# Wider weight loads in sixteen small matrix products, and seven more loop slots in written order

## The chip, the cores and the metric

The kernel runs on one NeuronCore of a Trainium2 chip. Its engines work side by side and meet only through semaphores: TensorE (PE, matrix products; the loading of its weights is listed apart as PEld), VectorE (DVE), ScalarE (ACT), GpSimd (POOL) and SyncE (SP, which issues most transfers). Each engine takes its own instructions strictly one after the other, in an order that is fixed when the program is built. The metric is the device time of one execution in microseconds; lower is better.

## The reference

Attention for 8 batches x 8 heads (512 local and 32 global positions each, 64 numbers a position), and then a two-layer network on all 4352 positions:

```python
s_l = scale * [q_l @ k_g.T, where(|i - j| <= 32, q_l @ k_l.T, -1e9)]   # local rows see a band and the 32 global keys
s_g = scale * q_g @ [k_g, k_l].T                                       # global rows see all keys
out = softmax(s) @ [v_g, v_l]          # for both
x = out rearranged to [B * 544, 512]
h = max(x @ w_in, 0)                   # 512 -> 2048
y = (h * h) @ w_out                    # 2048 -> 512
```

## The kernel before

The attention is cut into 128 tiles t: 16 groups of 256 query positions (half a batch), times 8 heads. The network is cut into 17 blocks of 256 positions with 8 steps m each (16 blocks of local positions; the last one holds the global positions). One loop (line 587) runs over both: its pass t, called **slot t** here and counted from 0, does the attention of tile t and finishes tile t-1, and does step m = t - 9 of the network. So slot 10 is the eleventh.

Tiles 0 to 15 are "plain" (line 82): their products take 32-bit numbers directly, which PE does in two passes a product. From tile 16 on, and from network block 1 on, every number is split into a high and a low part and each product becomes three; DVE and ACT make those parts.

A slot's work, in the order of the program text (lines 587 to 694): PE transposes the probabilities of tile t-1 (`pt`), does the first half of the network's first product (`h`, line 605); ACT copies `pt` (for plain tiles into `pts`, line 206); DVE masks the scores of tile t and takes their maximum (`softmax1`, a custom instruction in the profile, `prob<-s,con`); ACT does the exponentials (`softmax2`); the place 0 of the weight work; PE does the second half of `h` and the value products of tile t-1 (`av`, `xa<-pts,raw`), and for plain tiles the scores `s` of tile t+1; ACT does `relu` and `square` on `h` (`act1`, `r<-h` and `r<-r`) and copies the values out (`x_evac`, `x_h<-xa`), DVE takes the rest of them (`x_l`); DVE makes the reciprocal of the sums and ACT multiplies by it (`softmax3`; tiles 9 to 15 on ACT, line 192); place 1 of the weight work; for tile 16 on, `split_head(t+1)` (ACT `hi`, DVE `lo` and `hi`, line 125); place 2; the network's second product `o` of step m-1 on PE; place 3.

**Weight work.** The 32 weight chunks (512 KB each) come in by SP and must be unpacked: ACT makes `wf` from the raw words (`w_abs`, one instruction that is called "unpack" below, `wf<-wr`), DVE two steps on it (`w_bits`: a TENSOR_SCALAR and a SCALAR_TENSOR_TENSOR), and later ACT and DVE split the chunk for the later blocks (`w_split`: ACT `ws<-wf`, called "cast" below, DVE the remainder `ws<-wf,ws`). `PLAN` (line 30) says for each slot how many halves of `w_bits` (b) and how many splits (s) stand in its four places: slots 9 and 10 have eight b, slots 11 to 13 eight b and three or four s, slot 14 five b and four s, slots 15 and 16 five s, slots 17 to 22 two s each.

**What sets the order.** A scheduling layer orders the instructions on each engine when the program is built. `InOrder` (line 42) marks instructions so that they keep the order of the program text on their engine; `FREE = (17, 17, 17)` (line 31, used in line 589) says from which slot on this is so for DVE, ACT and PE. Before it, the layer may place an instruction where it likes, as long as the data allow it.

**Single buffers.** `pt`, `s` (from tile 8 on), `gs` and `xa` have one PSUM buffer each (line 78, `bufs=1`): the scores of tile t+1 can only be written when `softmax1` of tile t has read its own, and the next `pt` only when ACT has copied the last one.

Of the kernel before, what the change touches and what calls it, by code (L numbers as in the profile page):

```python
# [7 lines left out]
F32 = mybir.dt.float32  # L8
# [8 lines left out]
P = 128  # L17
HALF = 256
# [9 lines left out]
NPLAIN = 16  # L28

PLAN = [",,,b", "b,,,b", "b,,,b", "b,,b,", "b,,b,", "b,,b,", "b,,b,", "b,b,,b", "b,b,,b", "bb,bb,bb,bb", "bb,bb,bb,bb", "bbs,bb,bbs,bbs", "bbs,bbs,bbs,bbs", "bbs,bbs,bbs,bbs", "bbs,bbs,bs,s", "ss,s,s,s", "ss,s,s,s", "s,,s,", "s,,s,", "s,,s,", "s,,s,", "s,,s,", "s,,s,"]  # L30
FREE = (17, 17, 17)
LOOK = 2
SQ = (2, 3, 4, 5, 14, 15)
MUL = 9
# [24 lines left out]
def attention_moe(  # L59
# [18 lines left out]
    ps_a = ctx.enter_context(tc.tile_pool(name="ps_a", bufs=1, space=PSUM))  # L78
# [3 lines left out]
    def plain(t):  # L82
        return t < NPLAIN
# [141 lines left out]

    def av(t):
        hd = heads[t]
        xa = ps_a.tile([64, HALF], F32, tag="xa", name=f"xa{t}")
        c = QC + KC
        if plain(t):  # L230
            v, pts = hd["raw"][:, c:], hd["pts"]
            mm = [
                (xa, v[:, 192:256], pts[:, 256:512]),
                (xa[:, 0:128], v[:, 0:64], pts[:, 0:128]),
                (xa[:, 128:256], v[:, 64:128], pts[:, 128:256]),
            ]
        else:
            vh, vl, ph, pl = hd["hi"][:, c:], hd["lo"][:, QC:], hd["ph"], hd["pl"]
            mm = []
            for u in range(2):  # L240
                o, vs, ps = xa[:, 128 * u : 128 * u + 128], slice(64 * u, 64 * u + 64), slice(128 * u, 128 * u + 128)
                mm += [(o, vh[:, vs], ph[:, ps]), (o, vl[:, vs], ph[:, ps]), (o, vh[:, vs], pl[:, ps])]
            o = xa[:, 64:192]
            mm += [(o, vh[:, 128:192], ph[:, 256:384]), (o, vl[:, 128:192], ph[:, 256:384])]
            mm.append((xa, vh[:, 192:256], ph[:, 384:640]))
        for i, (o, a, b) in enumerate(mm):
            pe.matmul(o, a, b, start=i == 0, stop=i == len(mm) - 1, skip_group_check=True)
        hd["xa"] = xa

    def x_evac(t):  # L250
        g, h = divmod(t, 8)
# [335 lines left out]
    for t in range(NSTEP + LAG + 1):  # L587
        m = t - LAG
        ve.on, ac.on, pe.on = [t >= x for x in FREE]
        prev, run = 1 <= t <= NT, 0 <= m < NSTEP  # L590
# [33 lines left out]
        if prev:  # L624
            av(t - 1)
# [142 lines left out]
```

## Time and profile before

| | |
|---|---|
| median of 3 runs | 1073.95 us (1073.4 to 1074.8) |
| the profiled execution | 1073.67 us, of which 1071.9 us span from the first to the last instruction |
| PE busy | 1055.3 us, 98% of the span |
| DVE, ACT busy | 856.9 us (80%), 752.2 us (70%) |
| transfers | 96.78 MB; q1 packets take 27.1% of the 16 engines' span |
| granted PE clock | 1.000 |

Where the slots stand in the span (start of the transposes of a slot on PE): slot 9 at about 38.1 us, slot 10 at 42.7, slot 11 at 53.5, slot 12 at 63.3, slot 16 at 103.1, slot 17 at 112.2. Slots 10 to 16 are those that the change orders anew; seven of 137.

A row of the timeline reads: start in us, duration in us, engine, line, operation, out<-in, shapes, how many rows are merged into it, and in brackets the idle time before and what ended it. For matrix products the duration includes the draining of the array, so the pace of PE is read from one start to the next. Almost all instructions are issued by one helper (line 52), so they are told apart by their tiles.

### The profile page before, as it was taken

The page shows a single profiled execution, that of the slowest core. Times are in us where ns is not written, and L with a number is a line of the kernel's source. Part 1 is how long each engine was busy: PE and PEld are TensorE (multiplying, and loading weights), DVE is VectorE, ACT ScalarE, POOL GpSimd, SP SyncE. Part 2 cuts the span into 40 slices and gives each one's busy share as a digit, 9 for nine tenths or more (in the row PEclk, how much of TensorE's full clock was granted, in tenths as well). Part 3 has the DMA queues.
Part 4 walks back from the last instruction along what each step waited for, and adds up shares of the span by engine and source line. Part 5 has one row for each costly group of instructions (what it writes and reads, how often), then busy time and mean ns, then how long its engine had stood idle before and what let it go on. Part 6 is the DMA issues. An engine that isn't in the chain of part 4 may idle for free.

```text
span 1071.9 us, 21142 instructions
## 1 busy us (share of the span) xinstructions
PE 1055.3 (98%) x7568; PEld 939.3 (88%) x7568; DVE 856.9 (80%) x2687; ACT 752.2 (70%) x1901; POOL 3.9 (0%) x14
## 2 busy tenths in 40 slices
PE   7999999999999999999999999999999999999998
PEld 5676789998999899999998989998999999999896
DVE  4689889888888888888888889888888888884321
ACT  5789776778767776777777776777777787774322
POOL 1000000000000000000000000000000000000000
PEclk9999999999999999999999999999999999999999
DMA  9662222232322222223222222222322322201000
GB/s 372 265 256 92 83 82 82 75 91 76 93 70 82 85 82 66 89 66 102 75 90 65 84 84 82 76 79 83 94 74 69 87 93 65 88 29 34 13 20 20
DMA packets 54312, 96.78 MB, mean 90 GB/s; under 512 B 4288, under 2 KB 29376, under 8 KB 54208
## 3 DMA queue, kind: packets, MB, share of 16 engines
q1 hardware_dynamic: 53632, 94.95, 27.1%
q8 instruction: 60, 0.98, 0.4%
q10 hardware_dynamic: 576, 0.49, 0.2%
q14 instruction: 44, 0.36, 0.1%
HBM read 86.51 MB, written 8.91 MB: 89 GB/s over the span
## 4 chain that ended last, share of the span: by engine, by line
PE 88%; ACT 5%; DVE 3%; DMA 3%; issue 1%; SPq 0%
PE o L52 34%; PE h L52 33%; PE xa L52 7%; PE s L52 5%; PE pt L52 5%; PE gxo L52 2%; PE gs L52 2%; DMA wr<-in_w_dram 1%; DVE prob L52 1%; ACT r L52 1%; ACT ph L52 1%; DMA raw<-in_pk_dram 1%; ACT prob L52 1%; PE gt L52 1%; ACT hi L52 1%
## 5 line engine op out<-in xcount | busy, mean ns | idle before, releaser
L52 PE MATMUL h<-x_h,ws 128*128 128x256 f32 x2048 | 388.8, 283 | 0.0
L52 PEld LDWEIGHTS h<-x_h,ws 128*128 128x128 f32 x2048 | 327.0, 191 | 0.5
L52 PE MATMUL o<-ws,gh 128*128 128x512 f32 x1024 | 321.3, 395 | 0.0
L52 PE MATMUL h<-x_l,ws 128*128 128x256 f32 x1024 | 289.1, 282 | 0.1
L52 PEld LDWEIGHTS o<-ws,gh 128*128 128x128 f32 x1024 | 185.5, 188 | 34.6
L52 PE MATMUL o<-ws,gl 128*128 128x512 f32 x512 | 202.6, 396 | 0.0
L52 PEld LDWEIGHTS h<-x_l,ws 128*128 128x128 f32 x1024 | 195.8, 191 | 0.9 <-DVE x_l L52 0.4
L52 ACT CAST ph<-pt 128x256 fp32r<-128x256 f32 x448 | 141.1, 341 | 68.1 <-PE pt L52 61.2
L52 ACT ACTIVATE prob<-prob,st 128x224 f32<-128x224 f32 x270 | 127.7, 476 | 62.1 <-DVE st L52 60.1
L52 ACT ACTIVATE r<-h 128x512 f32<-128x512 f32 x136 | 81.4, 599 | 112.4 <-PE h L52 112.3
L52 PEld LDWEIGHTS o<-ws,gl 128*128 128x128 f32 x512 | 96.2, 188 | 22.7
L52 DVE CUSTOM_DVE_ANT_0 prob<-s,con 128x224 f32<-128x224 f32 x256 | 89.8, 386 | 25.6 <-PE s L52 19.5
L52 DVE TENSOR_TENSOR gl<-r,gh 128x512 fp32r<-128x512 f32 x128 | 87.9, 686 | 22.3 <-ACT gh L52 20.5
L52 ACT CAST hi<-raw 128x864 fp32r<-128x864 f32 x112 | 102.5, 915 | 1.3
L52 DVE TENSOR_TENSOR r<-h,r 128x512 f32<-128x512 f32 x82 | 56.7, 692 | 52.3 <-ACT r L52 51.0
L52 PE MATMUL xa<-ph,hi 128*64 128x128 f32 x448 | 87.3, 238 | 1.6 <-DVE ph L52 1.2
L52 DVE TENSOR_TENSOR hi<-raw,hi 64x352 fp32r<-64x352 f32 x224 | 82.5, 368 | 6.5
L52 ACT CAST gh<-r 128x512 fp32r<-128x512 f32 x128 | 79.1, 618 | 8.9 <-DVE r L52 8.6
L52 DVE TENSOR_TENSOR ph<-pt,ph 64x128 fp32r<-64x128 f32 x224 | 79.6, 356 | 7.0
L52 DVE TENSOR_TENSOR lo<-raw,hi 128x448 fp32r<-128x448 f32 x112 | 69.7, 622 | 15.2 <-ACT hi L52 12.5
L52 PE MATMUL pt<-con,prob 128*128 128x128 f32 (+1 forms) x512 | 77.9, 274 | 0.1
L52 DVE TENSOR_SCALAR prob<-prob,st 128x224 f32<-128x224 f32 x242 | 70.5, 334 | 4.2
(80 smaller groups left out, 1570.4 us busy)
## 6 DMA issues: line engine op xcount, KB each, us to landing
raw<-in_pk_dram SPq DMA_DIRECT2D x127, 432.0 KB, 3.3
wr<-in_w_dram SPq DMA_DIRECT2D x32, 512.0 KB, 7.4
gv<-in_vg_dram SPq DMA_DIRECT2D x32, 320.0 KB, 3.2
out_dram<-ot SPq DMA_DIRECT2D x32, 256.0 KB, 2.2
qr<-in_qg_dram SPq DMA_DIRECT2D x31, 64.0 KB, 2.7
out_dram<-ot SPq DMA_DIRECT2D x8, 64.0 KB, 1.7
raw<-in_pk_dram SPq DMA_DIRECT2D x1, 304.0 KB, 4.1
con<-in_consts_dram ACTq DMA_DIRECT2D x1, 224.0 KB, 3.9
```

The source lines that it names most:

```text
L52: r = method(*args, **kwargs)
```

## The change

Two edits.

1. For plain tiles, `av` loads 128 columns of weights in place of 64. The three products keep their moving operands and their places in the output, the output tile has 128 partitions, and only its first 64 are read. For this the value columns of the plain tiles are rolled by 64 in the host's packing of the input (what is multiplied is still the 32-bit value data; the extra 64 output rows are products with neighbouring columns that nobody reads).
2. `FREE` goes from 17 to 10 for all three engines.

```diff
-FREE = (17, 17, 17)
+FREE = (10, 10, 10)
...
     def av(t):
         hd = heads[t]
-        xa = ps_a.tile([64, HALF], F32, tag="xa", name=f"xa{t}")
         c = QC + KC
         if plain(t):
+
+            xa = ps_a.tile([P, HALF], F32, tag="xa", name=f"xa{t}")
             v, pts = hd["raw"][:, c:], hd["pts"]
             mm = [
-                (xa, v[:, 192:256], pts[:, 256:512]),
-                (xa[:, 0:128], v[:, 0:64], pts[:, 0:128]),
-                (xa[:, 128:256], v[:, 64:128], pts[:, 128:256]),
+                (xa, v[:, 0:128], pts[:, 256:512]),
+                (xa[:, 0:128], v[:, 64:192], pts[:, 0:128]),
+                (xa[:, 128:256], v[:, 128:256], pts[:, 128:256]),
             ]
         else:
+            xa = ps_a.tile([64, HALF], F32, tag="xa", name=f"xa{t}")
...
-        hd["xa"] = xa
+        hd["xa"] = xa[:64, :]
...
     pk[:NPLAIN, :64, c + 192 : c + 256] = pk[:NPLAIN, :64, c + 128 : c + 192]
+    pk[:NPLAIN, :, c:] = np.roll(pk[:NPLAIN, :, c:], 64, axis=-1)
```

What the second edit does to the order, at three places. In the names, the number behind a tile is its slot or chunk (`st10` is the softmax statistics of tile 10, `wr13` the raw words of chunk 13, `ws4` the split of chunk 4); the number after the underscore only tells buffers apart.

**DVE around the softmax of tile 10.** Before, from the last step on chunk 5:

```order
L52 SCALAR_TENSOR_TENSOR wf4_262<-wr5_260,wf4_262 128x512
L52 ISA prob0_93,st10_494<-s10_453,con_78 128x224
L52 ISA st10_494 128x1
L52 ISA prob0_93,st10_494<-s10_453,con_78 128x224
L52 ISA st10_494 128x1
L52 TENSOR_SCALAR st10_494<-st10_494 128x2
L52 TENSOR_SCALAR wf6_329<-wf6_329 128x512
L52 SCALAR_TENSOR_TENSOR wf6_329<-wr6_294,wf6_329 128x512
```

Now the same softmax stands further back. The piece begins with:

```order
L52 SCALAR_TENSOR_TENSOR wf4_262<-wr5_260,wf4_262 128x512
L52 TENSOR_SCALAR wf6_329<-wf6_329 128x512
L52 SCALAR_TENSOR_TENSOR wf6_329<-wr6_294,wf6_329 128x512
L52 TENSOR_TENSOR x_l_89<-xa8_449,x_h_88 64x256
L52 TENSOR_SCALAR wf6_329<-wf6_329 128x512
```

and, after the rest of chunk 7, chunks 8 to 11 and the first step of chunk 12, ends with:

```order
L52 SCALAR_TENSOR_TENSOR wf12_475<-wr12_466,wf12_475 128x512
L52 TENSOR_SCALAR wf12_475<-wf12_475 128x512
L52 ISA prob0_93,st10_494<-s10_453,con_78 128x224
L52 ISA st10_494 128x1
L52 ISA prob0_93,st10_494<-s10_453,con_78 128x224
L52 ISA st10_494 128x1
L52 TENSOR_SCALAR st10_494<-st10_494 128x2
L52 SCALAR_TENSOR_TENSOR wf12_475<-wr13_473,wf12_475 128x512
```

The softmax of tile 10 has moved behind chunks 6 to 12 and the first step of chunk 13, and behind `x_l` of tile 8.

**ACT at the head of slot 10.** Before:

```order
L52 ACTIVATE prob0_93,st10_494<-prob0_93,st10_494 128x224
L52 ACTIVATE r0_456<-h0_425 128x512
L52 CAST x_h_88<-xa8_449 64x256
L52 ACTIVATE r0_456<-r0_456 128x512
L52 COPY pts9_492<-pt_95 128x512
L52 ACTIVATE wf6_329<-wr7_327 128x512
```

Now, from the same `x_h` on:

```order
L52 CAST x_h_88<-xa8_449 64x256
L52 ACTIVATE wf6_329<-wr7_327 128x512
L52 ACTIVATE wf8_387<-wr8_361 128x512
L52 COPY sg_91<-gs8_402 64x160
L52 COPY sg_91<-gs8_402 64x96
L52 ACTIVATE wf8_387<-wr9_385 128x512
L52 ACTIVATE wf10_441<-wr10_417 128x512
L52 ACTIVATE wf10_441<-wr11_439 128x512
L52 ACTIVATE wf12_475<-wr12_466 128x512
L52 ACTIVATE wf12_475<-wr13_473 128x512
L52 COPY pts9_492<-pt_95 128x512
L52 ACTIVATE prob0_93,st10_494<-prob0_93,st10_494 128x224 x2
```

`sg` waits for PE's global scores of tiles 8 and 9, which PE now does in slot 10 after the transposes and the first half of `h` (before: behind the value products); the unpacking of chunks 9 to 13, the copy of `pt` and the exponentials of tile 10 stand behind it.

**DVE between slots 15 and 16.** Before, the split of head 16 began ahead of the softmax of tile 12:

```order
L52 SCALAR_TENSOR_TENSOR wf12_475<-wr13_473,wf12_475 128x512
L52 TENSOR_TENSOR lo16_946<-raw16_803,hi16_945 128x448
L52 ISA prob0_93,st12_643<-s12_585,con_78 128x224
L52 ISA st12_643 128x1
L52 ISA prob0_93,st12_643<-s12_585,con_78 128x224
```

Now it stands where the program text has it, two splits ahead of the softmax of tile 16:

```order
L52 TENSOR_TENSOR ws17_942<-wf16_542,ws17_942 128x512
L52 TENSOR_TENSOR lo16_946<-raw16_803,hi16_945 128x448
L52 TENSOR_TENSOR hi16_945<-raw16_803,hi16_945 64x352
L52 TENSOR_TENSOR hi16_945<-raw16_803,hi16_945 32x64
L52 TENSOR_TENSOR qgz_92<-qr16_953,qgz_92 128x2x2x32
L52 TENSOR_TENSOR ws18_961<-wf18_570,ws18_961 128x512
L52 TENSOR_TENSOR ws19_964<-wf18_570,ws19_964 128x512
L52 ISA prob0_93,st16_985<-s16_973,con_78 128x224
```

In slots 10 to 16 DVE, ACT and PE now follow the text slot by slot, as they do from slot 17 on in both kernels.

## The prediction

> **What bounds the kernel now.** I read the chain of waits first, then the busy time by stretch.
>
> ```profile
> PE 88%; ACT 5%; DVE 3%; DMA 3%; issue 1%; SPq 0%
> ```
> ```profile
> 31.70:112.70 81.00, 80.89 (x356) 55.73 (x357) 65.63 (x182) 68.46 (x162) 0.59 (x2) 1.00 0.50 188
> ```
> ```profile
> 112.70:146.00 33.30, 31.94 (x231) 27.15 (x230) 30.18 (x95) 28.29 (x69) 0.00 (x0) 1.00 0.21 65
> ```
>
> The columns are the stretch, its length, then busy time of PE, PEld, DVE, ACT and POOL. From 31.7 to 112.7 us, which holds the slots in question, PE is busy 80.89 of 81.00 us: it waits for nothing. DVE has 15 us to spare there, ACT 12.5. In the next stretch PE loses 1.4 us while DVE has only 3 us of 33 free: slots 17 to 20 are bound by DVE. So a gain on PE counts if DVE and ACT follow, and a delay of DVE at slot 17 goes to the end of the program undiminished.
>
> **The first edit: wider weights.** PE's rows in slot 13, and the same kind of `s` behind a `pt`:
>
> ```profile
> 76.12 1.46 PE L52 MATMUL h<-xg,wf 128*128 128x256 f32 x6
> 77.50 1.08 PE L52 MATMUL xa<-pts,raw 128*64 128x256 f32 x6
> 78.52 1.02 PE L52 MATMUL s<-raw 128*128 128x224 f32 x4
> 79.38 0.59 PE L52 MATMUL o<-wf,r 128*128 128x512 f32 x1
> ```
> ```profile
> 38.63 0.92 PE L52 MATMUL s<-raw 128*128 128x224 f32 x4
> 39.39 0.38 PE L52 MATMUL h<-xg,wf 128*128 128x256 f32 x1
> ```
>
> Behind `pt`, four rows of 224 columns take 39.39 - 38.63 = 0.76 us, 0.85 ns a column. By that pace the six `h` should take 1.30 (they take 1.38), the six `xa` (1024 columns) 0.87 (1.02), the `s` 0.76 (0.86): 0.33 us is lost at the two changes between 128 and 64 weight columns. With 128 everywhere I expect all of it back: 0.33 a slot. Slots 6 to 16 lie where PE sets the pace: eleven times 0.33 is 3.6 us. Before 31.7 us transfers set the pace, and I count nothing. Bounds: nothing, if the change of operands costs it and not the width, and 3.6.
>
> One rule speaks against the edit. The Trainium skill, "TensorE: Matmul & The Clock Gate", section "LDWEIGHTS (loading the stationary operand)", says that a load takes its number of columns divided by 1.2 in ns, so 107 for 128 columns and 53 for 64; were the 96 loads bare, that would be an estimated 5.1 us lost. The `s` rows above load 128 columns and keep to 0.19 us a row, so the trace shows such loads hidden.
>
> **The second edit: the jam at slot 10.** DVE must now finish chunk 12 and begin chunk 13 before it may do the softmax of tile 10, and PE cannot write `s` of tile 11 before that softmax, since `s` has one buffer.
>
> ```profile
> 41.71 0.43 DVE L52 TENSOR_SCALAR wf<-wf 128x512 int32<-128x512 int32 x1 [1.21 <-ACT wf L52]
> 42.17 0.69 DVE L52 SCALAR_TENSOR_TENSOR wf<-wr,wf 128x512 int32<-128x512 int32 x1
> 42.78 0.16 DVE L52 TENSOR_SCALAR st<-st 128x2 f32<-128x2 f32 x1
> ```
> ```profile
> 42.72 0.59 PE pt L52 x4
> ```
> ```profile
> 48.98 0.42 ACT L52 COPY sg<-gs 64x160 f32<-64x160 f32 x2
> ```
> ```profile
> 47.71 1.24 PE L52 MATMUL gs<-raw,qz 128*128 128x288 f32 x4
> 48.78 0.92 PE L52 MATMUL s<-raw 128*128 128x224 f32 x4
> ```
>
> A chunk costs DVE 0.46 + 0.61 = 1.07 us. Its start: slot 10 would begin about 0.9 earlier than its 42.7, at 41.8; transposes 0.44, half of `h` 1.73 and two global products 0.96 (all three by 0.85 ns a column) bring ACT's `sg` to 45.0, which blocks the unpacking of chunks 9 to 13 until 45.5; chunk 9 is unpacked at 46.2. Four chunks and the first step of chunk 13 (0.4): softmax of tile 10 at **50.9**. PE's `s` of tile 11 then starts at 51.6 and not at 48.78: 2.8 us later than before, the gains of slots 6 to 10 already in it.
>
> **The loop of slots 10 to 16.** In written order the two engines wait for each other in turn. Durations, from one start to the next, where the trace has this order already (slot 19), and from the weight work:
>
> ```profile
> 130.78 0.38 DVE L52 CUSTOM_DVE_ANT_0 prob<-s,con 128x224 f32<-128x224 f32 x1
> ...
> 144.26 0.16 DVE L52 TENSOR_SCALAR st<-st 128x2 f32<-128x2 f32 x1
> ...
> 144.66 0.58 DVE L52 TENSOR_SCALAR prob<-prob,st 128x224 f32<-128x224 f32 x2
> ```
> ```profile
> 131.72 0.48 ACT L52 ACTIVATE prob<-prob,st 128x224 f32<-128x224 f32 x1 [0.67 <-DVE st L52]
> ...
> 132.66 0.60 ACT L52 CAST ws<-wf 128x512 fp32r<-128x512 f32 x1
> 133.29 0.60 ACT L52 ACTIVATE r<-h 128x512 f32<-128x512 f32 x1
> 133.92 0.63 ACT L52 ACTIVATE r<-r 128x512 f32<-128x512 f32 x1
> 134.46 0.35 ACT L52 CAST x_h<-xa 64x256 fp32r<-64x256 f32 x1
> 134.71 0.91 ACT L52 CAST hi<-raw 128x864 fp32r<-128x864 f32 x1
> ```
> ```profile
> 91.38 0.69 ACT L52 ACTIVATE wf<-wr 128x512 f32<-128x512 f32 x1
> 91.97 1.64 ACT L52 CAST ws<-wf 128x512 fp32r<-128x512 f32 x3
> 93.52 0.67 ACT L52 ACTIVATE wf<-wr 128x512 f32<-128x512 f32 x1
> ```
> ```profile
> 44.60 0.84 ACT L52 ACTIVATE prob<-prob,st 128x224 f32<-128x224 f32 x2
> ```
> ```profile
> 91.06 0.42 DVE L52 TENSOR_SCALAR wf<-wf 128x512 int32<-128x512 int32 x1
> 91.39 0.69 DVE L52 TENSOR_TENSOR ws<-wf,ws 128x512 fp32r<-128x512 f32 x1
> 91.99 0.69 DVE L52 SCALAR_TENSOR_TENSOR wf<-wr,wf 128x512 int32<-128x512 int32 x1
> ```
> ```profile
> 118.52 0.40 DVE L52 TENSOR_TENSOR x_l<-xa,x_h 64x256 fp32r<-64x256 f32 x1
> 118.85 0.60 DVE L52 TENSOR_TENSOR lo<-raw,hi 128x448 fp32r<-128x448 f32 x1
> ...
> 120.28 0.45 DVE L52 TENSOR_TENSOR sg<-gs,sg 64x288 f32<-64x288 f32 x1
> ```
>
> From one softmax to the next in slot 12: softmax to exponentials 0.94 (130.78 to 131.72); exponentials 0.94; unpack 0.59; cast 0.52 (1.55 for three); `relu` 0.63; `square` 0.54; `x_h` 0.35; `x_l` 0.33 and the two small steps 0.40 (144.26 to 144.66); the multiplications 0.76 (0.84 less their overlap); then, in place 1, the next unpack and cast must end, 0.59 + 0.60, before DVE's remainder 0.60; places 2 and 3 keep DVE busy, 0.61 + 0.33 + 0.60 each. Sum: **10.9 us**.
>
> The other slots by the same rows. Slot 10 has no casts: 5.5 to the multiplications, then 0.69, 0.46, 0.61, 0.46, 0.61, 0.33 on DVE: 8.6. Slot 11 lacks the cast of place 1: 10.2. Slot 13 adds two remainders of the global probabilities ahead of the next softmax (a full and a small one, 1.0 by the rows of `ws`, `lo`): 11.9. Slot 14 has fewer halves, but a cast of `gv` on ACT: 10.2. Slot 15 has no unpacking, but the split of head 16 between `ws` steps (ACT 0.52 + 0.91, DVE 1.43 from 118.85 to 120.28): 10.2. Slot 16, with head 17 and the second `gv`: 9.4. Together **71.4**. PE's share is smaller:
>
> ```profile
> 53.64 0.44 PE pt L52 x4
> 63.42 0.44 PE pt L52 x4
> ```
>
> 9.78 us a slot, 9.45 without the lost 0.33. PE has no place in the loop: `r` and `x_h` find their products ready. So it waits, chiefly ahead of `pt` (for the multiplication), `s` (for the softmax) and, in slot 16, `s` of tile 16 (for the late split of its head).
>
> **The sum.** Softmax of tile 17 at 50.9 + 71.4 = 122.3. Before:
>
> ```profile
> 113.26 0.39 DVE L52 CUSTOM_DVE_ANT_0 prob<-s,con 128x224 f32<-128x224 f32 x1 [0.96 <-PE s L52]
> ```
>
> So DVE reaches its own bound stretch **9.0 us later**, and carries that to the end. PE's 0.33 a slot falls into waits from slot 10 on. 1073.67 + 9.0 = 1082.7 for the profiled execution; the median of the runs is 0.3 above it: **1083.0**. Bounds of the loop: 0.03 us at some nine handovers a slot, seven slots, are left out (+2); casts and unpacking that ACT does while it would wait may be ready earlier than I count (up to 0.5 a slot, -3.5). Own range 1079.5 to 1085.5.
>
> **The rivals.** *The order costs nothing.* If DVE and ACT keep to PE's 9.45 us, their 15 and 12.5 spare us suffice, and the 3.6 of the first edit come through: 1070.4. For it: totals of work are unchanged, and both engines have that room. Against it: it needs a loop 1.4 shorter than the sum of its rows, and PE to find `s` free at 48.5 where DVE has seven chunks to do first. It decides from loops below 9.45.
>
> *Only the jam costs.* Slot 10 throws PE back by 2.8, later loops fit behind PE, which wins back 0.33 in six slots: +0.8, so 1074.8. It needs the same short loop; for it, each slot has places where both engines could run ahead.
>
> *The width does not remove the loss.* Then slots 6 to 9 give 1.3 us less, but slots 10 to 16 stay bound by the loop; the jam's start moves by at most 0.9: 1083.9, inside my range.
>
> *The transfers fall behind.* Loads of raw words wait for buffers that DVE frees later. I see 0.50 of the transfer engines used from 31.7 to 112.7 us, and each chunk's load is due two chunks ahead, some 5 us of DVE work; a chunk late in each of slots 11 to 14 by 1 us would give 1087.
>
> **How the numbers follow.** Forecast with its near variants (width, bounds) 0.79; order free 0.09; only the jam 0.08; transfers 0.04. About 0.2% (2.1 us) is what a measurement can tell here. Faster: the free order and the low end of the jam case, 0.10; same (1071.8 to 1076.1): most of the jam case, 0.06; slower 0.84. The range reaches from the upper half of the jam case to the transfers' case: 1075.5 to 1087.5.
>
> **What would show it.** In the new profile: `h` to `xa` to `s` in slots 7 to 9 without the 0.33; softmax of tile 10 near 50.9; starts of the softmax of tiles 11 to 17 by 8.6 to 11.9 apart; PE idle ahead of `pt`, `s` and `xa`, with ACT and DVE as releasers, 9 us or more in all; the rest of the program shifted as a whole. Softmax starts 9.45 apart, or PE still busy throughout, would prove me wrong.

## The result, and the profile after

| | before | after |
|---|---|---|
| median of 4 runs each | 1074.14 us (1073.4 to 1074.8) | 1083.93 us (1083.74 to 1084.16) |
| ratio of the medians, 95% interval | | 1.0094 [1.0082, 1.0106] |
| the profiled execution, its span | 1073.67 us, 1071.9 us | 1084.08 us, 1082.3 us |

The change makes the kernel 9.8 us slower. The forecast was 1083.0, 0.9 too low. (The loop of line 587 has 146 slots; the order is new in seven of them.)

The chain of waits of the changed kernel, by engine. ACT and DVE now hold 17% of it, where they held 8%:

```profile
PE 80%; ACT 10%; DVE 7%; issue 2%; DMA 1%; ACTq 0%; POOL 0%; POOLq 0%
```

Busy time by stretch (columns as in the prediction). The first row holds slots 8 to 16 (slot 17 begins at 120.92 on PE, 8.75 us later than it did):

```profile
31.70:121.70 90.00, 82.00 (x358) 58.89 (x358) 65.33 (x177) 68.59 (x162) 0.59 (x2) 0.98 0.45 162
121.70:155.00 33.30, 31.50 (x225) 26.82 (x224) 30.75 (x96) 26.86 (x69) 0.00 (x0) 1.00 0.26 82
```

DVE's 65.3 and ACT's 68.6 us are the 65.6 and 68.5 of the 81 us before: the same work. It now takes 90 us, and PE, which waited for nothing there, is idle for 8.0 of them. So no engine has more to do; the three wait for each other.

Where they wait is read from the starts of the softmax on DVE in the timeline, here of tiles 10, 11 and 17 (start in us, duration; each is the first of two instructions); the table below has the distances of all eight:

```profile
50.87 0.38 DVE L52 CUSTOM_DVE_ANT_0 prob<-s,con 128x224 f32<-128x224 f32 x1
...
59.74 0.38 DVE L52 CUSTOM_DVE_ANT_0 prob<-s,con 128x224 f32<-128x224 f32 x1
...
123.76 0.38 DVE L52 CUSTOM_DVE_ANT_0 prob<-s,con 128x224 f32<-128x224 f32 x1
```

The softmax of tile 10 starts at 50.87 (before: 39.59), that of tile 17 at 123.76 (before: 113.26, so 10.5 later). Tile 18 is 10.25 later (132.23 against 121.98), and from there to the end of the program the delay stays between 10.2 and 10.6 but for one tile (10.7).

| softmax to softmax, from slot | 10 | 11 | 12 | 13 | 14 | 15 | 16 | sum |
|---|---|---|---|---|---|---|---|---|
| predicted | 8.6 | 10.2 | 10.9 | 11.9 | 10.2 | 10.2 | 9.4 | 71.4 |
| measured | 8.87 | 10.47 | 11.14 | 11.91 | 10.55 | 10.24 | 9.71 | 72.89 |

Beside the kernel before, this table does not yet show what the loop costs. There the softmax of tile 10 was done ahead of its slot (39.59; slot 10 began at 42.7), and from it to the softmax of tile 17 it was 73.67 us, no less than 72.89. The moves under "Shortening the loop" tell what the loop is worth and what the jam.

The chain in slot 12 (start, length, engine and tile; "issue" is time in which nothing that the profile shows was waited for; at 77.70 DVE is at the remainder `ws` that it began at 77.67) steps from ACT to DVE and back, and PE is not in it:

```profile
71.15 1.04 ACT prob L52 x4
72.20 0.58 ACT wf L52
72.77 0.51 ACT ws L52
73.28 0.50 ACT r L52
73.80 0.63 ACT r L52
74.46 0.37 ACT x_h L52
74.85 0.42 DVE x_l L52
...
75.70 0.85 ACT prob L52 x2
76.56 0.57 ACT wf L52
77.13 0.52 ACT ws L52
77.70 0.57 issue
78.28 0.51 DVE wf L52
```

And the waits of PE from 31 to 160 us (what waited, for whom, us in total, times, longest):

```profile
PE gs L52 <- DVE pth L52: 2.4, 1, 2.4
PE s L52 <- ACT ws L52: 1.7, 1, 1.7
PE s L52 <- DVE st L52: 1.4, 1, 1.4
PE gs L52 <- ACT sg L52: 1.3, 2, 0.8
PE s L52 <- DVE hi L52: 1.3, 1, 1.3
PE xa L52 <- ACT pts L52: 0.8, 1, 0.8
```

The first of them was not foreseen: in slot 14 PE's global scores `gs` wait for DVE to read the same single buffer (`pth`), and the second half of `h` stands behind them. In slots 11 and 12 PE does not wait at all and keeps its own pace; what DVE and ACT fall behind there comes out on PE in slots 14 and 16.

The first edit works. PE's slot 11 in the changed kernel:

```profile
57.52 0.60 PE L52 MATMUL pt<-con,prob 128*128 128x128 f32 x4
57.96 1.89 PE L52 MATMUL h<-xg,wf 128*128 128x256 f32 x8
...
61.90 1.04 PE L52 MATMUL xa<-pts,raw 128*128 128x256 f32 x6
62.78 0.92 PE L52 MATMUL s<-raw 128*128 128x224 f32 x4
63.53 3.60 PE L52 MATMUL o<-wf,r 128*128 128x512 f32 x8
66.97 0.60 PE L52 MATMUL pt<-con,prob 128*128 128x128 f32 x4
```

`xa` takes 62.78 - 61.90 = 0.88 from start to start (it took 1.02), `s` 0.75 (0.86), and the slot 66.97 - 57.52 = 9.45, as forecast. The gain is there and is swallowed by the waits.

### The profile page after: what moved, and what is told of

Same layout as the page of the kernel before. It is cut to its first block, busy times and chain, and to the rows that moved or that the text cites. A ratio compares the mean times of both kernels' runs of the same rounds, so it can differ in the third digit from the quotient of the medians.

```text
span 1082.3 us, 21134 instructions
## 1 busy us (share of the span) xinstructions
PE 1056.3 (98%) x7568; PEld 944.0 (87%) x7568; DVE 859.1 (79%) x2687; ACT 752.2 (70%) x1901; POOL 3.9 (0%) x14
## 4 chain that ended last, share of the span: by engine, by line
PE 80%; ACT 10%; DVE 7%; issue 2%; DMA 1%; ACTq 0%; POOL 0%; POOLq 0%
PE o L52 30%; PE h L52 30%; PE xa L52 6%; PE s L52 5%; PE pt L52 4%; ACT prob L52 2%; PE gxo L52 2%; DVE prob L52 2%; PE gs L52 2%; ACT r L52 2%; DVE wf L52 1%; DVE ws L52 1%; ACT hi L52 1%; ACT ph L52 1%; DVE st L52 1%
## 5 line engine op out<-in xcount | busy, mean ns | idle before, releaser
L52 DVE TENSOR_TENSOR lo<-raw,hi 128x448 fp32r<-128x448 f32 x112 | 69.7, 622 | 15.5 <-ACT hi L52 12.6
```

The lines of the kernel that those rows point to most:

```text
L52: r = method(*args, **kwargs)
```

## The experiments

All times are medians, with the ratio to the kernel before (95% interval) from the same chip. The kernel before has medians of 1073.45 to 1074.14 us on the chips that were used, so a difference between two kernels from different chips is uncertain by up to 0.7 us. The theory: the second edit makes the whole loss, through a jam at slot 10 and then a loop of DVE and ACT that is longer than PE's slot; the first edit gains, but only where PE sets the pace. The rivals: the width costs; PE's own order costs; only the jam costs.

### Each edit alone

The first edit alone: the changed kernel with

```diff
-FREE = (10, 10, 10)
+FREE = (17, 17, 17)
```

> Only the first edit: value products with 128 weight columns, FREE stays (17, 17, 17). Theory (the lost 0.33 us a slot comes back, and slots 6 to 16 are bound by PE when DVE and ACT may run ahead): 3.6 us faster than before, about 1070.4 us by the median, with h to xa to s about 0.3 us shorter a slot and PE without waits from 31.7 to about 109 us. Rival (the change of operands costs it, not the width): 1074 us, no change. Rival (wider loads are not hidden): up to 1079 us.

Measured: **1071.49 us**, 0.9981 [0.9972, 0.9990]. It gains 2.0, not 3.6. Slot by slot on PE (start of `pt` to start of `pt`, this kernel less the kernel before): slots 1 to 5 together -0.48, slot 6 -0.05, slot 7 -0.16, slot 8 -0.41, slot 9 0, slot 10 -0.15, slots 11, 12 and 13 -0.33, -0.33, -0.34, slot 14 **+0.37**, slot 15 -0.33, slot 16 -0.13. That is -2.34, less 0.37 because slot 1 began later in this execution. In slot 14 a wait shows that had been covered by slower products:

```profile
87.33 0.75 PE L52 MATMUL gs<-raw,qz 128*128 128x288 f32 x2 [0.54 <-DVE pth L52]
```

The end of the loop follows: the softmax of tile 17 starts at 111.28 instead of 113.26. So the width gains 0.33 or more in five of the eleven slots. In the others a wait takes some or all of it, most of them too short for the list of waits: in slot 7 the first weight load of `xa` waits for ACT's `pts`, in slot 6 the next `pt` waits 0.16 for DVE, and in slots 9, 10 and 16 `h`, `gs` and `s` start 0.15 to 0.19 later behind the row before them than they did.

The second edit alone: the changed kernel with `av` and the packing as before.

```diff
-                (xa, v[:, 0:128], pts[:, 256:512]),
+                (xa, v[:, 192:256], pts[:, 256:512]),
... the other products and the packing likewise
```

> Only the second edit: FREE = (10, 10, 10), value products with 64 weight columns as before. Theory (slots 10 to 16 are bound by the loop between DVE and ACT, so PE's width does not matter there, and slots 6 to 9 only move the start of the jam, by at most 0.9 us): 1083.9 to 1085 us, starts of the softmax of tiles 10 to 17 the same distances apart as with both edits (8.9, 10.5, 11.1, 11.9, 10.6, 10.2, 9.7). Rival (the wide loads make part of the loss): clearly below the changed kernel, 1075 to 1082 us.

Measured: **1085.72 us**, 1.0114 [1.0100, 1.0128]; the rival falls. Softmax of tile 10 at 51.89, 1.0 later than with both edits (at most 0.9 was expected), and then the distances 8.87, 10.47, 11.13, 11.91, **11.88**, 10.24, 9.71: the same but for slot 14, which is 1.3 longer. There the granted clock (third column from the end) fell after PE's wait for `pth`:

```profile
92.00:94.00 2.00, 0.00 (x0) 0.00 (x0) 1.97 (x5) 1.11 (x3) 0.00 (x0) 1.00 0.00 0
94.00:96.00 2.00, 1.71 (x6) 1.46 (x7) 1.11 (x6) 0.79 (x3) 0.00 (x0) 0.85 0.00 0
96.00:98.00 2.00, 2.00 (x6) 1.07 (x5) 1.04 (x3) 1.95 (x5) 0.00 (x0) 0.50 0.00 0
```

By the medians the first edit is thus worth 1.8 us in the changed kernel; in the profiled executions tile 17 is 2.3 later, 1.0 by the start of the jam and 1.3 in slot 14, where `h` and `xa` run at half the clock. The profiled execution is the slowest of its four runs (1086.93), so the clock may not have fallen there in all of them.

### 96 columns

The first edit alone, with 96 weight columns:

```diff
-            xa = ps_a.tile([P, HALF], F32, tag="xa", name=f"xa{t}")
+            xa = ps_a.tile([96, HALF], F32, tag="xa", name=f"xa{t}")
...
-                (xa, v[:, 0:128], pts[:, 256:512]),
-                (xa[:, 0:128], v[:, 64:192], pts[:, 0:128]),
-                (xa[:, 128:256], v[:, 128:256], pts[:, 128:256]),
+                (xa, v[:, 0:96], pts[:, 256:512]),
+                (xa[:, 0:128], v[:, 64:160], pts[:, 0:128]),
+                (xa[:, 128:256], v[:, 128:224], pts[:, 128:256]),
```

> As the first edit alone, but value products with 96 weight columns (xa has 96 partitions). It tells what the lost 0.33 us at the changes of width hangs on. If narrower loads than the array's full 128 columns lose time at each change, the six xa rows take near 1.02 us from the first to the next product and the s behind them 0.86, as with 64 columns: PE's slots 11 and 12 are 9.78 us, the kernel about 1073.5 us. If only 64 columns and fewer do: 0.88 and 0.76, slots of 9.45 us, about 1071.5 us as with 128.

```profile
62.20 0.60 PE L52 MATMUL pt<-con,prob 128*128 128x128 f32 x4
...
66.58 1.03 PE L52 MATMUL xa<-pts,raw 128*96 128x256 f32 x6
67.44 0.92 PE L52 MATMUL s<-raw 128*128 128x224 f32 x4
...
71.64 0.60 PE L52 MATMUL pt<-con,prob 128*128 128x128 f32 x4
```

Measured: **1071.52 us**, 0.9978 [0.9967, 0.9988]; `xa` 0.86 from start to start, the slot 9.44. Of the three widths only 64 loses time at the changes; a mismatch of 96 to 128 does not. The rows of the weight loads (PEld) show where it is lost. With 64 columns the first load of `xa` starts only with its product (77.50 in slot 13 before), after 0.33 without a load. The same gap stands in slot 12, there with "issue" as what ended it, so it is not a wait for ACT:

```profile
77.50 0.84 PEld L52 LDWEIGHTS xa<-pts,raw 128*64 128x64 f32 x6 [0.33 <-ACT ws L52]
```

With 128 columns it starts 0.21 ahead of the product (66.21 and 66.42 in slot 12 of the first edit alone), with 96 columns 0.22 ahead (66.36 and 66.58). The load of the `s` behind it likewise starts with its product (78.52) after the 64 columns, and 0.10 ahead of it after 128 or 96. Why a load at a change to or from 64 columns does not run ahead, no run shows.

### The written order on one engine, or two

`FREE` lists DVE, ACT and PE. All four kernels below have the first edit.

```diff
-FREE = (10, 10, 10)
+FREE = (17, 17, 10)      # PE alone in written order
```

> Both edits, but the written order for PE alone from slot 10 on: FREE = (17, 17, 10). Theory (the order on DVE and ACT makes the loss): near the first edit alone, 1070 to 1072 us. Rival (PE's own written order is the cause, its products standing behind ones whose inputs come late): about 1083 us.

```diff
-FREE = (10, 10, 10)
+FREE = (10, 17, 17)      # DVE alone
```

> Both edits, but the written order for DVE alone from slot 10 on: FREE = (10, 17, 17). Theory (the loop takes two: DVE waits for ACT and ACT for DVE in turn; an ACT that may run ahead has the exponentials and unpacked chunks ready, and its sg no longer stands ahead of the unpacking): less than half of the changed kernel's loss, 1072 to 1078 us, softmax starts 9.5 us or less apart after a shorter jam. Rival (DVE's order alone is enough, since it holds the softmax behind the weight work): 1082 to 1084 us.

```diff
-FREE = (10, 10, 10)
+FREE = (17, 10, 17)      # ACT alone
```

> Both edits, but the written order for ACT alone from slot 10 on: FREE = (17, 10, 17). Theory (the loop takes two): less than half of the loss, 1072 to 1078 us. Rival (ACT's order alone is enough, above all sg ahead of five unpackings in slot 10): 1082 to 1084 us.

```diff
-FREE = (10, 10, 10)
+FREE = (10, 10, 17)      # DVE and ACT
```

> Both edits, but the written order for DVE and ACT alone from slot 10 on, PE free until slot 17: FREE = (10, 10, 17). Theory (the loop between DVE and ACT has no place for PE): as the changed kernel, 1083 to 1084 us, with the same distances of the softmax starts. Rival (PE's order is the cause): about 1071 us.

| written order from slot 10 on | median | ratio to before | against the first edit alone |
|---|---|---|---|
| none (first edit alone) | 1071.49 | 0.9981 [0.9972, 0.9990] | |
| PE | 1072.96 | 0.9994 [0.9985, 1.0004] | +1.5 |
| ACT | 1074.81 | 1.0008 [0.9999, 1.0018] | +3.3 |
| DVE | 1077.89 | 1.0037 [1.0023, 1.0052] | +6.4 |
| DVE and ACT | 1087.00 | 1.0124 [1.0110, 1.0138] | +15.5 |
| all three (the change) | 1083.93 | 1.0094 [1.0082, 1.0106] | +12.4 |

PE's order is not the cause (its kernel is 1 us above the range that was expected for it). DVE alone and ACT alone cost 9.7 us together, both at once 15.5: the loop takes two. With DVE alone in order the softmax distances are 8.0, 9.7, 9.6, 10.1, 7.6, 7.3 and 8.0; the expected shorter jam did not come (the softmax of tile 10 starts at 57.5), and three of the distances are above the expected 9.5, but PE has other work ready meanwhile and waits for nothing from 41 to 63 us.

DVE and ACT in order without PE was expected at 1083 to 1084 and is 3 us above. The distances are the same to 0.05 (8.92, 10.47, 11.13, 11.89, 10.56, 10.25, 9.70); two other places pay. A PE that may run ahead does all of `h` and part of `o` before the global scores, so ACT's `sg`, with the unpacking behind it, comes at 48.14 instead of 45.25:

```profile
48.14 0.42 ACT L52 COPY sg<-gs 64x160 f32<-64x160 f32 x2 [4.22 <-PE gs L52]
```

That puts the softmax of tile 10 at 52.69, 1.8 later. And in slot 17, after a wait of 3.8 us, PE runs at half the clock:

```profile
120.42 1.15 PE L52 MATMUL pt<-con,prob 128*128 128x128 f32 x4 [3.80 <-DVE prob L52]
```
```profile
120.00:124.00 4.00, 1.90 (x7) 1.43 (x8) 3.67 (x8) 3.95 (x9) 0.00 (x0) 0.50 0.00 0
124.00:128.00 4.00, 4.00 (x20) 4.00 (x20) 3.81 (x14) 2.18 (x8) 0.00 (x0) 0.50 0.66 192
```

The softmax of tile 18 follows that of tile 17 after 9.67 instead of 8.47, 1.2 more. Together 3.0. So PE's written order helps the changed kernel, by 1.8 at the jam, since it brings `gs` forward.

### Shortening the loop

The changed kernel with the weight work of place 3 in place 0:

```diff
-  ... "bb,bb,bb,bb", "bbs,bb,bbs,bbs", "bbs,bbs,bbs,bbs", "bbs,bbs,bbs,bbs", "bbs,bbs,bs,s", ...
+  ... "bbbb,bb,bb,", "bbsbbs,bb,bbs,", "bbsbbs,bbs,bbs,", "bbsbbs,bbs,bbs,", "bbss,bbs,bs,", ...
```

> The changed kernel with the weight work of place 3 moved into place 0 in slots 10 to 14 (PLAN rows bbbb,bb,bb, and bbsbbs,bb,bbs, and bbsbbs,bbs,bbs, twice and bbss,bbs,bs,): the same work, no instruction more or less. Theory (the sum of the loop: place 3 is 1.54 us of DVE ahead of the next softmax, in place 0 it lies partly beside the exponentials and costs 1.1 more of ACT's unpack and cast): each of the five loops about 0.4 shorter, together 2 us less than the changed kernel, about 1082 us. Rival (what counts is the total of weight work, or transfers): 1084 us, no change. Rival (work in place 0 stands ahead of the exponentials' users): longer than 1085 us.

Measured: **1082.19 us**, 1.0078 [1.0063, 1.0093], 1.7 below the change. The distances are 8.37, 10.03, 10.68, 11.45, 10.55, 10.24, 9.70: the first four shorter by 0.50, 0.44, 0.46 and 0.46 where the sum of rows said 0.43. Slot 14 was expected to shrink too and did not. The chain of the changed kernel shows why: there DVE's work of place 0, behind the remainder of `gv`, stands on the chain ahead of `x_l`, so that a remainder moved to place 0 stays on it.

```profile
95.90 0.69 DVE gvl L52
...
96.94 1.03 DVE wf L52 x2
97.96 0.60 DVE ws L52
...
98.60 0.42 DVE x_l L52
```

So the same work in another place moves the loop by what its rows say, where the chain is the one that was summed.

The softmax of tiles 11 to 15 ahead of place 3:

```diff
-        if live:
+        if live and not 11 <= t <= 15:
             softmax1(t)
+        if live:
             softmax2(t)
...
+        if 11 <= t + 1 <= 15:
+            softmax1(t + 1)
         w_tick(t, 3)
```

> The changed kernel with the softmax of tiles 11 to 15 written ahead of place 3 of the slot before it, so that ACT gets its scores 1.54 us of DVE work earlier. Theory (the loop is the sum of its rows): the loops into tiles 11 to 15 shrink towards PE's 9.45, five times 0.5 to 1.5, and of the loss mainly the jam and slots 15 and 16 are left: 1075 to 1079 us. Rival (only the jam costs, or DVE's total does): 1083 to 1084 us, no change.

Measured: **1082.13 us**, 1.0076 [1.0061, 1.0091]: only 1.8 below the change, a miss. Up to the softmax of tile 14 the distances are 7.80, 8.93, 9.78 and 9.51, together 6.4 less (1.5 of it is the new place of the softmax itself). Slot 14 gives much of it back: 13.50 to the softmax of tile 15, where it was 10.55.

```profile
89.92 0.75 PE L52 MATMUL gs<-raw,qz 128*128 128x288 f32 x2 [2.42 <-DVE pth L52]
90.51 2.98 PE L52 MATMUL h<-xg,wf 128*128 128x256 f32 x8
93.29 1.67 PE L52 MATMUL xa<-pts,raw 128*128 128x256 f32 x6
94.80 0.92 PE L52 MATMUL s<-raw 128*128 128x224 f32 x4
```
```profile
92.00:94.00 2.00, 2.00 (x6) 1.64 (x5) 0.57 (x1) 0.47 (x1) 0.00 (x0) 0.50 0.55 164
```

With the shorter loop PE does stand in it in slot 14: DVE's `pth` lets PE's `gs` go, the second half of `h` stands behind, at half the clock, and ACT's `relu` and `x_h` wait for PE. Two kernels take this apart. In the first PE has work in that wait:

```diff
         if run:
             gemm1(m, 0)
+        if t == 14:
+            gemm1(m, 0)
```

> The kernel with the early softmax of tiles 11 to 15, and in slot 14 the first half of h computed twice (the same 8 products again, 1.73 us of PE work that nothing needs), so that PE has work while its gs waits for DVE's pth. In that kernel the granted clock fell to 0.50 after this wait and PE took about 1.5 us longer for h, xa and s, which stood on the chain of waits. If the wait brings the clock down: clock 1.00 from 88 to 100 us, slot 14 on PE 13.2 instead of 14.7 us, the kernel 1.0 to 1.5 us faster than without the added products, about 1080.9 us. If something else lowers the clock, or PE is not on the path there: 1082 us or, with 1.7 us more work, up to 1083.9 us.

```profile
92.00:94.00 2.00, 2.00 (x10) 1.71 (x10) 1.94 (x5) 0.37 (x1) 0.00 (x0) 1.00 0.05 16
```

Measured: **1081.16 us**, 1.0065 [1.0048, 1.0081]. The wait is 0.62 instead of 2.42, the clock stays at 1.00, and the distance is 12.22 instead of 13.50. The median is 1.0 lower, as expected, but that is not clear of noise: the runs overlap (1079.8 to 1081.7 against 1080.9 to 1082.7, on different chips), and the two profiled executions took the same time (1081.68 and 1081.63). What the one with the added products gains in slot 14 it loses in slots 11 and 12 (9.53 and 10.07 instead of 8.93 and 9.78): there the clock had fallen behind the waits of slot 10, with PE on the chain. That the wait in slot 14 brought the clock down agrees with this; one execution of each does not show it, as the last section tells.

In the second `gs` goes behind `h`, `xa` and `s` in slot 14:

```diff
-        if live and early:
+        if live and early and t != 14:
             g_scores(t)
...
         if early and t + 1 < NPLAIN:
             scores(t + 1)
+        if t == 14:
+            g_scores(t)
```

> The kernel with the early softmax of tiles 11 to 15, and in slot 14 the global scores gs (which wait for DVE's pth, since gs has one buffer) written behind the second half of h, the value products and the scores of tile 15, instead of ahead of them. If the miss of the early softmax (1082.1 us, not 1075 to 1079) comes from that one place, where PE stands in the loop: softmax of tile 15 about 9.5 to 10 us behind that of tile 14 instead of 13.5, the kernel 3 to 4 us faster, 1078 to 1079 us. If the early softmax gains nothing because DVE's total or the jam sets the end: 1082 us.

Measured: **1078.96 us**, 1.0047 [1.0032, 1.0062], with slot 14 at 10.71. With `gs` out of the way the early softmax gains 5.0, and that one place had held 3.2 of them, the lowered clock included.

At last the softmax of tile 10 early as well:

```diff
-        if live and not 11 <= t <= 15:
+        if live and not 10 <= t <= 15:
...
-        if 11 <= t + 1 <= 15:
+        if 10 <= t + 1 <= 15:
```

> The same with the softmax of tile 10 early too (written in slot 9, ahead of its place 3, where the order is still free), which takes the jam of slot 10 apart: the four chunks stay ahead of the softmax of tile 11, but no exponentials and no scores wait for them. Theory (the jam holds PE and ACT, not only DVE): softmax of tile 11 at about 54.8 instead of 58.3 us, the kernel 3 to 3.5 us faster than with gs late alone, about 1075 us, near the kernel before. If the backlog of chunks on DVE is what costs, whatever stands behind it: softmax of tile 11 at 58 us, no gain, 1078 to 1079 us.

```profile
39.79 0.38 DVE L52 CUSTOM_DVE_ANT_0 prob<-s,con 128x224 f32<-128x224 f32 x1
...
56.43 0.38 DVE L52 CUSTOM_DVE_ANT_0 prob<-s,con 128x224 f32<-128x224 f32 x1
```

Measured: **1075.80 us**, 1.0020 [1.0011, 1.0029]: 3.2 less. The softmax of tile 10 is back at 39.79 and that of tile 11 at 56.43 (58.98 without; 54.8 was expected).

Three moves in the program text, with no instruction more or less, thus take back about 8 of the 9.8 us. Still 4.3 above the first edit alone, this kernel loses on PE, against that one, 1.6 in slot 10, 1.1 in slot 16 (`s` waits 1.3 for the late split of head 16) and 0.8 in slot 17 (`s` behind ACT's `ws`, 1.1). The first edit alone, with 128 columns or with 96, stays the fastest of all kernels here, 0.2% below the kernel before.

## Why the prediction was right, point by point

**What bounds the kernel.** Right: a delay of DVE at tile 17 goes to the end all but undiminished (10.25 us at tile 18, 10.2 to 10.7 behind it).

**The width.** Right in size: 0.33 a slot, PE's slots 11 and 12 at 9.45. Right that the order swallows it, but for the start of the jam and slot 14. The 3.6 that it gave the edit alone was too high: 2.0 came. The step that failed is that PE sets the pace in all of slots 6 to 16: slots 6, 7, 9, 10, 14 and 16 gave less or nothing, since waits of 0.15 to 0.54 came out from behind the slower products. The rule on weight loads that would have cost an estimated 5.1 us, from the Trainium skill, "TensorE: Matmul & The Clock Gate", section "LDWEIGHTS (loading the stationary operand)", does not decide here: in the slots without waits the loads run beside the products before them (the first load of `xa` starts 0.21 ahead of its product).

**The jam.** Right within 0.3 us at every step: slot 10 starts at 41.91 (41.8 predicted), `sg` is copied from 45.25 (45.0), DVE begins chunk 9 at 46.27 (46.2), the softmax of tile 10 starts at 50.87 (50.9), and `s` of tile 11 at 51.62 (51.6). The start of slot 10 is in part luck: the prediction took it from the gains of slots 6 to 10, but slots 6 to 9 are only 0.51 shorter than before and slots 1 to 5, for which nothing was counted, 0.48. Its price, as far as the early softmax of tile 10 undoes it, is 3.2 us.

**The loop.** The mechanism was right and the term too small: 72.9, not 71.4. Five of the seven distances are 0.24 to 0.35 above the sum of their rows and two within 0.04. The sum left out the handovers between the engines: it named some nine a slot of 0.03 each, +2 for seven slots as a bound. They are only a part of the miss. The chain of waits from the softmax of tile 10 to that of tile 17 has 20 handovers, some three a slot, 0.47 us in all; 32 gaps of the same size (0.81) stand between instructions of one engine, and rows that are read from start to start hold some of these already. The rest of the 1.5 is not taken apart here, and the agreement of some terms is luck: in slot 14 the chain is another than in slot 12 and goes through DVE's `gvl` and the weight work of place 0, and not through `relu`, `square` and `x_h`. The other bound, engines running ahead (-3.5), did not show in the changed kernel: no distance is shorter than its sum.

**PE has no place in the loop.** True of the changed kernel, whose chain has no piece of PE from the softmax of tile 10 to that of tile 17, and true only as long as the loop is as long as it is. In slot 14 `gs` waits for DVE and holds up `h`; the prediction named no such wait, though it is PE's longest (2.4). In the kernels with only the order or with the early softmax it is on the chain. This wait is what the working lacked.

**The sum.** 9.0 was forecast for tile 17 and 10.5 came; 0.25 of it is won back by tile 18. Of the 0.9 by which the forecast is low, the loop's 1.5 are more than enough, less what DVE's own stretch wins back and the spread between executions (the distance of the two spans is 10.4, of the medians 9.8). The own range does not add up: 1083.0 and the bound of 2 give 1085.0 at the top, not 1085.5; the measured time lies inside either.

**The rivals.** *The order costs nothing* falls by the second edit alone, 12.3 us slower than the kernel before on the same chip. *Only the jam costs* falls by the moves that shorten the loops at an unchanged jam (place 3: -1.7, and 1.9 in its distances; early softmax with late `gs`: -5.0). *The width does not remove the loss* falls by PE's rows, but its time, 1083.9, was what the kernel took: a time alone would not have told it from the forecast. *The transfers fall behind* falls: none of PE's waits from 31 to 160 us in the changed kernel is for a transfer, nor is any of ACT's or DVE's from 31 to 125 us.

## What to carry to other kernels

Spare time in totals does not protect an order: DVE and ACT had 15 and 12.5 us free in 81, and lost 10 as soon as each had to do its work in the order of the text, through a jam at the first slot and because one round through both engines (8.9 to 11.9 us) was in six of seven slots longer than PE's 9.45. Add up the round, instruction by instruction, with 0.02 to 0.03 us for each gap between two instructions of the chain, before fixing an order; then look for what every engine has queued behind its waits, and move the wait behind the work, as `gs` here (3.2 us) or the softmax (1.8 and 3.2). When a bound goes away, as PE's narrow products did, the next wait stands close behind: of 3.6 us 2.0 were left.

## What the runs showed of the hardware

**The clock can fall after short waits.** In the changed kernel the granted clock is 0.50 from 52 to 54 us, after PE had waited 0.51, 0.84 and 1.44 us within 7 us. It cost nothing that the distances show: with the second edit alone the clock stays at full behind the same three waits (0.51, 0.85, 1.48), and the next two distances are the same (8.87 and 10.47). The early softmax has a single wait of 2.42 us with the clock at 0.50 behind it, 1.7 us of PE time on the chain (from `h` to `s` 4.29, in the changed kernel's slot 14 2.61). In slot 14 of the changed kernel two waits (0.84 and 2.35 us) leave the clock at full:

```profile
93.28 0.75 PE L52 MATMUL gs<-raw,qz 128*128 128x288 f32 x2 [2.35 <-DVE pth L52]
```

while with the second edit alone, after 0.84 and 2.36, it fell. In a fourth kernel, with DVE alone in written order, it stayed at 1.00 behind a wait of 2.41. So of the four traces with a wait of 2.35 to 2.42 us the clock fell in two. That is why the full clock of the one execution with eight added products is no proof that they kept it up; the mean granted clock of all four runs, 0.997 to 1.000 with them and 0.996 to 0.997 without, points the same way. The Trainium skill, "TensorE: Matmul & The Clock Gate", Part 1 (The HAM clock gate), tells of an activity window of about 3.4 us that runs freely and of half the clock after an idle window. That the same waits end in one way or the other agrees with a window that runs freely. The rule that the page draws from it (section "HAM oscillation — how this bites in real kernels"), no idle gaps of more than about 3.4 us, is too mild here: 2.4 us was enough in two of four cases.

**A load that has to wait shows.** In slot 2 the first weight load of `xa` waits for ACT's `pts`. From the first `xa` to the first `s` it is then 0.98 us with 128 columns:

```profile
19.12 1.14 PE L52 MATMUL xa<-pts,raw 128*128 128x256 f32 x6 [1.08 <-ACT pts L52]
20.10 0.55 PE L52 MATMUL s<-raw 128*128 128x224 f32 x2
```

and 1.01 with 64:

```profile
18.76 1.08 PE L52 MATMUL xa<-pts,raw 128*64 128x256 f32 x6 [0.81 <-ACT pts L52]
19.77 0.65 PE L52 MATMUL s<-raw 128*128 128x224 f32 x2
```

In the flow the wide form takes 0.88 and the narrow one 1.02. So behind a wait 0.03 is left of the 0.14 that `xa` gains. It is the same 0.98 in slot 7 of the first edit alone, where PE itself shows no wait and only its load does (0.31 for `pts`).

**Width.** The two changes between 128 and 64 weight columns in a slot cost 0.33 us, where the loads start with their products and not ahead of them; those between 128 and 96 cost nothing that can be seen.
